# The first expert product of an attention and soft-MoE kernel, moved to a PSUM bank of the output's pool

## The chip, the cores and the metric

The kernel runs on one core of a Trainium2 chip. The metric is the device time of one execution in microseconds (us). The times shown are medians of three runs.

## The reference

The reference is an attention layer whose output goes straight into a soft mixture of experts:

```
# q, k, v: (4, 8, 768, 64); attention in a band of 31 keys, plus 24 block summaries (maximum of k, mean of v)
x = attention(q, k, v)                     # reshaped to (3072, 512)
logits = x @ phi                           # (3072, 32): 8 experts x 4 slots
d = softmax(logits, axis=0); c = softmax(logits, axis=1)
slot_input = d.T @ x                       # (32, 512)
for e in range(8):
    h = maximum(slot_input[4e:4e+4] @ w1[e], 0)    # w1[e]: 512 x 1024
    slot_out[4e:4e+4] = h @ w2[e]                  # w2[e]: 1024 x 512
out = c @ slot_out                         # (3072, 512)
```

All inputs are float32. w1 and w2 are 16 MB each, and the output is 6 MB.

## The kernel before

The program has two parts. The first runs over 24 steps of attention (`for i in range(NSTEP)`); between the steps of attention, pieces of the routing are placed by two tables written out by hand (`PLAN`, and `TAIL` for what follows the last step). Each engine executes its instructions in the order in which the code writes them; the framework adds the waits on semaphores.

In the first part the eight banks of PSUM belong to four pools: `ps_t` (two banks, tag "pt"), `ps_o` (one tile of two banks), `ps_s` (two) and `ps_p` (two). After the last step `att.close()` gives them back. The second part opens two new pools of four banks each, `pf` and then `po`. The banks of `pf` are those of `ps_t` and `ps_o`; the banks of `po` are those of `ps_s` and `ps_p`. The first tile taken from a new pool waits for the instructions that used the old pools whose place it takes.

The end of the first part, in the order of `TAIL`: the last routing sums (`route_d`, accumulated by VectorE into `acc` on line 414); `lanes` (lines 420 to 439), whose last matmul (438) leaves a column in a tile `pp` of `ps_p`; `slots` (441 to 454), which multiplies `acc` into the slot inputs (445), copies them into the stationary operand `W1ST` (449, VectorE) and makes the reciprocal `rz` from the column of line 438 (453, 454); and `row_exp(1)` (457 to 471), which transposes the last two blocks of logits into the tile `o` of `ps_o` (463, TensorE), takes their row maxima (468, VectorE), subtracts them (469, VectorE) and takes the exponent (471, ScalarE).

The second part begins with `row_split` (629 to 638: VectorE and ScalarE make the combine weights `cr`), and beside it the first expert product on TensorE: 32 pieces of w1 of 512 KB each, four matmuls a piece, all accumulated into one tile `hps` (lines 652 to 665). After each piece `load_piece()` issues the DMA of the piece that takes its place, on the queue of SyncE; 43 pieces lie on the chip at that time (`NPRE`), so that pieces 43 to 63 come in while the first 21 are used up. Then follow the maximum with zero (668, 669), transposes of `cr` (`pair_up`, tiles `pc` of `po`) and of the hidden layer (`ph` of `pf`), and a hand-written interleave `ENDING` of the four column blocks of the second product (`stage2`, line 690, tiles `so` and `so2` of `pf`) with the combine (`combine`, line 717, tiles `op` of `po`), whose results VectorE and ScalarE copy to `ot` (726) and SyncE stores (728).

The lines of `slots` and `row_exp` that the prediction speaks of:

```
nc.vector.tensor_copy(out=W1ST..., in_=pi...)                                # 449
nc.vector.tensor_scalar_add(out=rz, in0=ps["z"][:, 0:1], scalar1=EPS)        # 453
nc.vector.reciprocal(out=rz, in_=rz)                                         # 454
nc.tensor.transpose(pv[:, 128 * q : 128 * q + 128], ltq[q0 + q], ident)      # 463
nc.vector.reduce_max(out=cm, in_=lv, axis=AX)                                # 468
nc.vector.tensor_tensor(out=c, in0=lv, in1=cm..., op=ALU.subtract)           # 469
```

Of the kernel before, what the change touches and what calls it, by code (L numbers as in the profile page):

```python
# [9 lines left out]
F32 = mybir.dt.float32  # L10
# [70 lines left out]
def attention_soft_moe(  # L81
# [534 lines left out]
    pf = ctx.enter_context(tc.tile_pool(name="pf", bufs=4, space=PSUM))  # L616
    po = ctx.enter_context(tc.tile_pool(name="po", bufs=4, space=PSUM))
# [11 lines left out]
    def row_split(q0, n):  # L629
        cm = fin.tile([128, 4 * n], F32, name=f"cm{n}", bufs=1)  # L630
        c = lt_all[:, q0 : q0 + n].rearrange("p q (g s) -> p (q g) s", s=NS)
        nc.vector.reduce_sum(out=cm, in_=c, axis=AX)
        nc.vector.tensor_scalar_add(out=cm, in0=cm, scalar1=EPS)
        nc.vector.reciprocal(out=cm, in_=cm)
        nc.vector.tensor_tensor(out=c, in0=c, in1=cm.unsqueeze(2).broadcast_to([128, 4 * n, NS]), op=ALU.mult)
        both = cr[:, 4 * q0 : 4 * q0 + 4 * n]
        nc.scalar.copy(out=both[:, :, 0, :], in_=c)
        nc.vector.tensor_tensor(out=both[:, :, 1, :], in0=c, in1=both[:, :, 0, :].bitcast(F32), op=ALU.subtract)
# [10 lines left out]

    row_split(0, 4)  # L650
    row_split(4, 2)
    hps = pf.tile([128, 512], F32, name="hps", tag="pf")[:, 0:256]
    for k in range(32):
        _, e, c = pieces[k]
        t = wt[k].rearrange("p (j f) -> p j f", j=4)
# [167 lines left out]
```

## Time and profile before

| | |
|---|---|
| median of three runs | 195.24 us (194.88, 195.24, 196.53) |
| the profiled execution: device time | 194.91 us |
| the profiled execution: span of the trace | 193.1 us |
| TensorE busy (matmul) | 169.9 us, 88% of the span |
| VectorE, ScalarE, GpSimd busy | 115.1, 92.1, 78.7 us |
| moved by DMA | 67.64 MB, mean 350 GB/s |

The span runs from the first to the last instruction; the device time holds 1.8 us more. Engines in the profile: PE is TensorE's matmul, PEld its loads of stationary operands, DVE is VectorE, ACT ScalarE, POOL GpSimd, SPq SyncE's queue. "PEclk" is the share of its full clock that TensorE was granted. A row of the timeline has the start, the duration, engine, line, operation, and tiles as output<-inputs; "x8" counts the records that were merged. A float32 matmul leaves two records, so that the 128 matmuls of line 657 are 256 records, eight for each piece of w1. In brackets stands how long the engine was idle before, and what released it; "issue" is idle time in which it waited for nothing that the profile shows.

### The profile page before, as it was taken

The numbers are of one execution on the slowest core, as the hardware profiler recorded it, in microseconds if no ns is written. First come the engines' busy times: TensorE is split into PE (matmuls) and PEld (weight loads), VectorE is DVE, ScalarE is ACT, GpSimd is POOL, SyncE is SP. The second block draws the span as 40 slices with busy tenths as digits, with TensorE's granted clock in tenths as the row PEclk, the third lists the DMA queues.
The fourth block names the chain that finished last, engine by engine and source line by source line (L and its number), as shares of the span: only waits on it lengthen the run. The fifth ranks groups of instructions, "written<-read, shape, count | busy, mean of one in ns | idle before, by whom it ended". The sixth has DMA issues, their size and how long they took to land.

```text
span 193.1 us, 7825 instructions
## 1 busy us (share of the span) xinstructions
PE 169.9 (88%) x3163; PEld 128.7 (67%) x3163; DVE 115.1 (60%) x580; ACT 92.1 (48%) x202; POOL 78.7 (41%) x106
## 2 busy tenths in 40 slices
PE   7779899899799999799989999999879997889950
PEld 5537668677658778578856877876636667768720
DVE  2539959749629958868958867657573020143460
ACT  2036657658464775756686475847220031033440
POOL 2048766856645666576666465860010000000000
PEclk9999999999999999999999999999859999999996
DMA  6999999999998899999899976975959999987696
GB/s 211 351 415 418 416 414 417 419 415 413 404 416 342 277 398 418 410 377 354 247 395 392 392 236 238 311 267 204 333 193 316 417 420 415 416 319 303 259 393 260
DMA packets 19331, 67.64 MB, mean 350 GB/s; under 512 B 2144, under 2 KB 2528, under 8 KB 19296
## 3 DMA queue, kind: packets, MB, share of 16 engines
q1 hardware_dynamic: 19296, 67.15, 90.3%
q8 instruction: 25, 0.41, 0.8%
q14 instruction: 10, 0.08, 0.1%
HBM read 60.85 MB, written 6.29 MB: 348 GB/s over the span
## 4 chain that ended last, share of the span: by engine, by line
PE 60%; DVE 11%; issue 8%; DMA 8%; ACT 5%; POOL 3%; SPq 2%; POOLq 0%; ACTq 0%; DVEq 0%
PE o L309 9%; PE hps L657 8%; PE so L690 8%; DMA v<-vx 8%; PE pt L286 7%; PE s L253 6%; PE pp L208 5%; PE op L717 4%; DVE p L271 3%; DVE kh L184 3%; PE pp L399 2%; PE pp L356 2%; POOL p L275 2%; PE pp L340 2%; PE pp L224 1%
## 5 line engine op out<-in xcount | busy, mean ns | idle before, releaser
L275 POOL TENSOR_TENSOR p<-p,m 128x480 f32<-128x480 f32 x48 | 46.3, 986 | 23.3 <-DVE m L271 22.9
L271 DVE CUSTOM_DVE_ANT_0 p<-s,cs 128x120 f32<-128x120 f32 x192 | 41.0, 278 | 4.9 <-PE s L253 3.5
L280 ACT ACTIVATE p<-p 128x480 f32<-128x480 f32 x48 | 29.0, 608 | 21.8 <-POOL p L275 21.6
L235 POOL COPY v<-vsst 24x520 f32<-24x520 f32 x47 | 29.1, 620 | 20.2 <-issue 17.9
L291 ACT COPY ptr<-pt 120x512 f32<-120x512 f32 x48 | 26.5, 588 | 20.8 <-PE pt L286 20.3
L309 PEld LDWEIGHTS o<-v,ptr 120*64 120x64 f32 x736 | 24.0, 137 | 9.6 <-issue 4.1
L309 PE MATMUL o<-v,ptr 120*64 120x65 f32 x736 | 27.4, 225 | 1.7 <-issue 1.2
L286 PE MATMUL pt<-ident,p 128*120 128x128 f32 x192 | 27.3, 280 | 1.2 <-ACT p L280 1.1
L253 PE MATMUL s<-k,q 64*64 64x120 f32 x768 | 25.9, 269 | 2.1 <-DMA q<-qx 1.2
L253 PEld LDWEIGHTS s<-k,q 64*64 64x64 f32 x768 | 20.3, 133 | 6.1 <-issue 1.7
L286 PEld LDWEIGHTS pt<-ident,p 128*120 128x120 f32 x192 | 20.3, 137 | 6.0 <-ACT p L280 3.3
L184 DVE TENSOR_REDUCE kh<-k 128x30 f32<-128x480 f32 (+1 forms) x32 | 16.1, 545 | 3.4 <-DMA k<-kx 3.4
L657 PE MATMUL hps<-w,W1ST 128*32 128x256 f32 x256 | 15.8, 413 | 1.1 <-DVE lt_all L469 1.1
L329 DVE TENSOR_TENSOR x<-o,z 128x512 f32<-128x512 f32 x23 | 15.9, 691 | 0.8
L271 DVE DVE_READ_ACCUMULATOR2_ANT m<- 128x1 f32 x192 | 15.9, 83 | 0.0
L726 DVE COPY ot<-op 128x512 f32<-128x512 f32 x12 | 7.9, 688 | 11.6 <-PE op L717 11.6
L690 PE MATMUL so<-w,W1ST 128*32 128x128 f32 x256 | 13.4, 275 | 1.0 <-issue 1.0
L657 PEld LDWEIGHTS hps<-w,W1ST 128*32 128x32 f32 x256 | 9.2, 119 | 7.6 <-issue 3.1
L208 PE MATMUL pp<-v,cs 120*32 120x256 f32 x192 | 12.6, 384 | 1.9 <-DMA v<-vx 1.1
L690 PE MATMUL so<-w,W2ST 128*32 128x128 f32 x256 | 13.1, 273 | 0.0
L340 PE MATMUL pp<-ident,x 128*128 128x128 f32 x88 | 12.5, 274 | 0.3 <-ACT xt L346 0.3
L346 ACT COPY xt<-pp 128x512 f32<-128x512 f32 x21 | 12.1, 602 | 0.1
(112 smaller groups left out, 181.2 us busy)
## 6 DMA issues: line engine op xcount, KB each, us to landing
w<-w SPq DMA_DIRECT2D x64, 512.0 KB, 8.9
v<-vx SPq DMA_DIRECT2D x24, 520.0 KB, 7.7
k<-kx SPq DMA_DIRECT2D x16, 472.0 KB, 7.6
q<-qx SPq DMA_DIRECT2D x12, 512.0 KB, 7.0
out<-ot SPq DMA_DIRECT2D x10, 512.0 KB, 3.6
out<-ot SPq DMA_DIRECT2D x4, 256.0 KB, 3.4
cs<-cst SPq DMA_DIRECT2D x1, 288.0 KB, 6.2
self__116<-selx SPq DMA_DIRECT2D x1, 64.0 KB, 5.9
```

The source lines that it names most:

```text
L184: nc.vector.reduce_max(out=kh[:, pr, :, n0 : n0 + m], in_=v[:, :, c0 : c0 + 16 * m].rearrange("p j (m k) -> p j m k", k=16), axis=AX,)
L208: nc.tensor.matmul(pv[32 * g : 32 * g + 32, 0:256], lhsT=cs[0:U, ic : ic + 32], rhs=v[0:U, ab, tt, :, 0:64], start=(tp == 0), stop=(tp == ...
L235: eng.tensor_copy(out=v, in_=src)
L253: nc.tensor.matmul(ps_[i, ab][h : h + 64, u, :], lhsT=qt[i // 2][rows, c : c + 64], rhs=kt[hb, pr][rows, k0 : k0 + U], start=True, stop=Tr ...
L271: nc.vector.tensor_tensor_reduce(out=p[:, n, :], in0=ps_[i, ab][:, 2 * tt + pr, :], in1=maskv[:, mk, :], scale=-0.125, scalar=-NEG, op0=AL ...
L275: nc.gpsimd.tensor_tensor(out=p, in0=p, in1=m.unsqueeze(2).broadcast_to([128, 4, U]), op=ALU.subtract)
L280: nc.scalar.activation(out=p, in_=p, func=AF.Exp, scale=-1.0)
L286: nc.tensor.transpose(pt[:, n, :], p[:, n, :], ident)
L291: nc.scalar.copy(out=ptr, in_=ptr_[i, tt])
L309: nc.tensor.matmul(o[64 * ab : 64 * ab + 64, h, :], lhsT=ptr[:, 2 * pr + ab, 64 * (r ^ ab) : 64 * (r ^ ab) + 64], rhs=v[0:U, ab, tt, h, :] ...
L657: nc.tensor.matmul(hps[32 * j : 32 * j + 32, :], lhsT=W1ST[:, c, 28 * e : 28 * e + 32], rhs=t[:, j, :], start=(k == 0), stop=(k == 31), ti ...
L690: nc.tensor.matmul(so[32 * j : 32 * j + 32, :], lhsT=W2ST[i][:, j, 28 * e : 28 * e + 32], rhs=t[:, i, j, :], start=(e == 0 and i == 0), st ...
```

## The change

The tile `hps`, into which the first expert product accumulates, is taken from the pool `po` (under the tag of the output's tiles) and no longer from `pf`:

```
-    hps = pf.tile([128, 512], F32, name="hps", tag="pf")[:, 0:256]
+    hps = po.tile([128, 512], F32, name="hps", tag="op")[:, 0:256]
```

No instruction is added, removed or moved on any engine. What differs are waits. On TensorE, at the beginning of the first expert product (W1ST is the slot inputs, w_204 the first piece of w1):

```order
 L438 MATMUL pp<-stat,R 128x1 [waits DVE_49,PE_49]
 L463 MATMUL o<-ident,lt_all 128x128 x2
-L657 MATMUL hps<-w_204,W1ST 32x256 [waits DVE_49,PE_49,Pool_49]
+L657 MATMUL hps<-w_204,W1ST 32x256 [waits DVE_49,Pool_49]
 L657 MATMUL hps<-w_204,W1ST 32x256 x3
 L657 MATMUL hps<-w_286,W1ST 32x256 x4
```

The first matmul of the product no longer waits for TensorE's own transposes of line 463 to complete, and its wait for VectorE, which keeps its name, is for another instruction: the count before is reached with line 469, the count now with line 453, three instructions earlier in VectorE's order, which is the same before and after:

```order
540 L414 SCALAR_TENSOR_TENSOR acc<-acc,st,tl 128x256
541 L382 SCALAR_TENSOR_TENSOR stat<-stat,st 128x1
542 L449 COPY W1ST<-tl 128x32x4 [waits DMAHW2_49,DMAHW7_49,PE_49,Pool_49]
543 L453 TENSOR_SCALAR rz<-pp 128x1 [waits PE_49]
544 L454 RECIPROCAL rz<-rz 128x1 [waits DVE_49]
545 L468 TENSOR_REDUCE kh<-o 128x8 [waits PE_49]
546 L469 TENSOR_TENSOR lt_all<-o,kh 128x256 [waits DVE_49]
547 L632 TENSOR_REDUCE cm_2706<-lt_all 128x16 [waits DVE_49]
```

Line 453 is the last reader of a tile of `ps_p`, line 469 the last of a tile of `ps_o`. Later, the tiles of `pf` and `po` fall on other banks by one place in the rotation. On TensorE in the third column block of the combine, this exchanges the waits of two matmuls that follow each other; nothing else differs:

```order
 L717 MATMUL op<-cT,sl 128x512 [waits DVE_49]
 L717 MATMUL op<-cT,sl 128x512
-L717 MATMUL op<-cT,sh 128x512 [waits Activation_49]
-L717 MATMUL op<-cT,sh 128x512 [waits DVE_49]
+L717 MATMUL op<-cT,sh 128x512 [waits DVE_49]
+L717 MATMUL op<-cT,sh 128x512 [waits Activation_49]
 L717 MATMUL op<-cT,sl 128x512 x2
```

## The prediction

> **What bounds the kernel now.** I read the chain that ended last first, then the timeline and the clock around the place of the change, then DMA from there to the end. From the page:
>
> ```profile
> span 193.1 us, 7825 instructions
> PE 60%; DVE 11%; issue 8%; DMA 8%; ACT 5%; POOL 3%; SPq 2%; POOLq 0%; ACTq 0%; DVEq 0%
> ```
>
> TensorE carries the chain. The same chain, cut to the passage into the second part, in order of time (start, duration, what):
>
> ```profile
> 139.36 0.38 PE pp L438 x2
> 139.74 0.54 PE o L463 x2
> 140.28 0.02 issue
> 140.31 0.44 DVE kh L468
> 140.74 0.02 issue
> 140.77 0.44 DVE lt_all L469
> 141.20 0.14 issue
> 141.34 15.82 PE hps L657 x256
> ```
>
> Here the chain leaves TensorE, goes through two VectorE instructions that make softmax weights, and comes back for the expert product. The product reads nothing of what they write. The timeline has the details:
>
> ```profile
> 139.46 0.29 DVE L449 COPY W1ST<-tl 128x128 f32<-128x128 f32 x1 [1.19 <-issue]
> 139.60 0.67 PE L463 MATMUL o<-ident,lt_all 128*128 128x128 f32 x2
> 139.78 0.16 DVE L453 TENSOR_SCALAR rz<-pp 128x1 f32<-128x1 f32 x1
> 140.77 0.42 DVE L469 TENSOR_TENSOR lt_all<-o,kh 128x256 f32<-128x256 f32 x1
> 141.34 1.51 PE L657 MATMUL hps<-w,W1ST 128*32 128x256 f32 x12 [1.07 <-DVE lt_all L469]
> ```
>
> The operand W1ST is ready at 139.46 + 0.29 = 139.75. TensorE ends its transposes at 139.60 + 0.67 = 140.27, stands idle for 1.07 us, and starts when line 469 (done at 141.19) releases it. So this one wait bounds the start.
>
> **What the change takes away.** The product now waits for line 453, done at 139.78 + 0.16 = 139.94. From the end of line 469 to the first matmul it took 141.34 - 141.19 = 0.15; by the same step the release comes at 139.94 + 0.15 = 140.09. TensorE takes its instructions in order, so that the transposes of line 463 are still ahead. Their modelled end is 140.27, but a matmul starts before the end of the one ahead: line 463 began at 139.60, while these rows let line 438 end later.
>
> ```profile
> 139.18 0.57 PE L438 MATMUL pp<-stat,R 128*128 128x1 f32 x2
> ```
>
> It ended at 139.75, 0.15 after its successor's start. With the same overlap the product starts at 140.27 - 0.15 = 140.12; without any, and with the full 0.15 of a release behind the end, at 140.42. I take **140.12**, since the nearest pair of rows shows the overlap: the start moves by 141.34 - 140.12 = **1.22 us** (0.92 to 1.25 by the ends). What is late next is TensorE's own work; line 453 and W1ST are both ahead of it.
>
> **What the gain is worth at the end of the product.** It starts on a slowed clock. Rows of 0.25 us each (stretch, length, PE busy, granted clock, DMA share, GB/s), and the loads of the product:
>
> ```profile
> 138.00:138.25 0.25, 0.25 (x4) 0.91 1.01 410
> ...
> 140.75:141.00 0.25, 0.00 (x0) 0.50 1.06 426
> ...
> 145.00:145.25 0.25, 0.25 (x8) 0.93 0.80 131
> ...
> 189.25:189.50 0.25, 0.00 (x0) 0.81 1.03 426
> ...
> 141.74 0.23 PEld L657 LDWEIGHTS hps<-w,W1ST 128*32 128x32 f32 x4 [0.20 <-issue]
> 142.17 0.22 PEld L657 LDWEIGHTS hps<-w,W1ST 128*32 128x32 f32 x4 [0.20 <-issue]
> ...
> 145.10 11.57 PEld L657 LDWEIGHTS hps<-w,W1ST 128*32 128x32 f32 x216
> ```
>
> The clock drops where a stretch is partly at 1 and partly at 0.5: 0.91 puts the drop 0.205 into its stretch, at 138.205; by the same working the clock comes back at 145.035 and drops again at 189.405. On half clock four records take 142.17 - 141.74 = 0.43, or 0.107 each; on the full one 11.57 / 216 = 0.0536. Before, 141.34 to 145.035 holds 3.70 / 0.107 = 34.5 records, and the other 221.5 take 11.87 us.
>
> So it matters whether the clock's return moves with the start. The three changes lie 6.83 and 44.37 us apart, and 44.37 / 6.83 = 6.50: they fit a beat of 3.41 us, with return and drop on it. If the beat has another phase against the program in every execution, then on the mean over executions the return follows the start of steady work: earlier work finds an earlier beat, and the whole product moves by the full 1.22 us. That is what I take for a median over runs. The times of before fit it: where a beat falls, the slow part is longer by up to 3.41 us, which costs half of that, 1.7 us; the three runs lie 196.53 - 194.88 = 1.65 us apart. The profiled run is at their lower end and had a favourable beat: 145.035 - 3.415 = 141.62, 0.28 us after the product began.
>
> The Trainium skill bears on this: the page "TensorE: Matmul & The Clock Gate", section "What's actually happening", says that the clock is judged over a free-running window of 3413 ns and that one busy window gives the full rate back. The trace agrees with the length (6.83 is twice 3.41). It speaks against counting the whole move in any single run; what it would make of the profiled phase is the first rival.
>
> **From the product to the end.** Everything up to the last matmul follows the product on TensorE. Three things might give the time back. Pieces of w that come too late: SyncE's queue waited for the product itself, so that its DMAs move with it.
>
> ```profile
> SPq L145 <- PE hps L657: 7.3, 9, 4.5
> L145 SPq DMA_DIRECT2D w<-w x29: 327/328/508, 125.9 to 163.4; - x29
> DMA to landing us min/median/max: 3.3/9.0/11.3
> ```
>
> The last piece is issued at 163.4 and lands by 163.4 + 11.3 = 174.7, while the last column block of the second product runs after 177 (row below); the cover is over 2 us, and grows when SyncE issues earlier. The order on SyncE stays, and the outputs queue behind the pieces as now. DMA bandwidth:
>
> ```profile
> 144.00:171.00 27.00, 24.62 (x518) 17.65 (x510) 4.64 (x14) 3.55 (x9) 0.00 (x0) 0.98 1.01 398
> 171.00:177.00 6.00, 6.00 (x144) 4.64 (x142) 2.38 (x6) 2.02 (x5) 0.00 (x0) 1.00 0.77 300
> 177.00:183.00 6.00, 6.00 (x143) 4.64 (x142) 2.49 (x6) 2.05 (x5) 0.00 (x0) 1.00 0.67 268
> 188.00:193.10 5.10, 0.00 (x0) 0.00 (x0) 0.00 (x0) 0.00 (x0) 0.00 (x0) 0.64 0.68 272
> ```
>
> It is full (1.01) while the pieces come, and free for 6 x (0.23 + 0.33) = 3.4 us after them, which is enough for 1.2. The last outputs drain behind the last matmuls, and so move along. Third, TensorE has two stalls whose cause no row names:
>
> ```profile
> 163.73 0.30 PE L690 MATMUL so<-w,W1ST 128*32 128x128 f32 x2 [1.04 <-issue]
> 169.74 0.51 PE L717 MATMUL op<-cT,sl 64*128 64x512 f32 x2 [1.34 <-issue]
> q8 instruction: 1, 0.02, 1.5%
> ```
>
> In the stretch from 160 to 163.8 one packet of the queue for instructions moved (last row). I read both stalls as TensorE waiting for its own code, on DMA that is full of weights. Pieces and product move together, so I leave both at their size; the bounds are that they vanish (a gain of 1.04 + 1.34 = 2.38 more) or that a third one of 1.34 appears; I take nothing, between the two, as the stretch's DMA share is what it was.
>
> The other edits of waits cost nothing: the exchange in the combine stands between two matmuls whose tiles VectorE and ScalarE free in the same pair of copies, and the tiles `ph` and `so` of `pf` come up some 16 us after line 469. VectorE, ScalarE and GpSimd wait for what they waited for before.
>
> **The sum.** Profiled execution: 194.91 - 1.22 = 193.69, with the clock's return moved along. That execution lies 0.33 below the median of 195.24, so for a median I put 195.24 - 1.22 = **194.0 us**.
>
> **The rivals.**
>
> *The clock keeps its beat, and half the gain is lost.* With the return at 145.035 and the start at 140.12, 4.92 / 0.107 = 46.0 records run slowly and the other 210 take 11.26: the end moves from 156.91 to 156.30, a gain of 0.61. Time 194.3 to 194.6 (from the profile and from the median). For it: the beat above. Against: the phase changes, and a median sees many.
>
> *The clock returns a beat earlier.* Before, the beat from 138.2 to 141.62 had an idle stretch of 1.07 us in it and did not bring the clock back. Without that hole TensorE is busy through it. If that is enough, only 1.50 / 0.107 = 14 records are slow, the other 242 take 12.97, and the product ends at 154.59: a gain of 2.32. Time 192.6 to 192.9. Against: line 445's and 438's small matmuls fill half of that beat, and the beat before it, from 134.8, was also busy for two thirds and yet cost the clock.
>
> *The change doesn't do what it says:* the product starts at 141.3 all the same, because a wait that I take for done (W1ST's clearing by GpSimd, the first pieces of w) is not. No row speaks for it. Time 194.9 to 195.2.
>
> *Slower: code comes later.* If the second product reaches its stretches of code earlier than the weights have left DMA, each later stretch adds a stall like the 1.04 and 1.34 above (1.19 in the mean). In the chain, between the two stalls:
>
> ```profile
> 163.73 1.06 PE so L690 x27
> 164.79 0.42 PE so L703 x2
> 165.21 2.76 PE so L690 x96
> 167.97 0.43 PE op L717 x2
> ```
>
> These are 27 + 2 + 96 + 2 = 127 records of matmul; two more such stretches fit into the span before the last matmul, near 175 and 181. Both would cost 2.4, against 1.2 gained: 195.24 + 1.2 = 196.4. It decides where DMA's share at these places is near 1 instead of 0.77 and 0.67. Against: the weights are issued earlier too.
>
> **How the numbers follow.** The forecast 0.45; beat kept 0.22; a beat earlier 0.15; no effect 0.08; code later 0.06; 0.04 for what I don't see. The range reaches from the beat earlier, 192.6, to no effect, 195.3: it leaves out the slower case and the unseen (the stalls gone among it), and allows for where three runs fall on the beat. A change within 1% (1.95 us) can't be told from none here. Faster by more needs 193.29 or less, which is the beat earlier and a little of the forecast's own lower side: 0.18. Slower by over 1% (197.2) needs the code's stalls and a bad beat: 0.03. The rest, 0.79, is within 1%.
>
> **What would show it.** In the profile after, the first matmul of line 657 at 140.1, with no idle time put down to line 469; VectorE's lines 468 and 469 where they were, beside the product; the clock's return somewhere between 141.6 and 147; the product's end near 156 (earlier by what the clock allows); the two stalls still there with 1.0 to 1.4 us; the last copy of line 726 as much earlier as the product's end. I would be wrong if the product began on time and its end did not move, or if the stalls of "issue" grew by as much.

## The result

The changed kernel takes 193.59 us (median of 20 runs, 190.48 to 195.59), the kernel before 195.34 us (20 runs, 192.78 to 197.01): 1.75 us or 0.9% less. The ratio of the two is 0.9865 with a 95% interval of 0.9828 to 0.9901; it is lower than the ratio of the medians (0.9910) because it compares only the executions of each kernel that lie close to its own fastest.

The profiled execution took 192.18 us, 2.73 less than the one before. The chain that ended last, at the same place, in order of time (start, duration, what):

```profile
138.32 0.30 DVE R L434
138.62 0.04 issue
138.67 1.08 PE tl L445 x8
139.75 0.20 PE pp L438 x2
139.94 0.28 PE o L463 x2
140.22 0.12 issue
140.34 14.02 PE hps L657 x256
154.36 1.02 PE pc L645 x8
```

VectorE's lines 468 and 469 are gone from the chain. In the timeline they run beside the product:

```profile
139.81 0.41 PE L463 MATMUL o<-ident,lt_all 128*128 128x128 f32 x2
139.84 0.29 DVE L449 COPY W1ST<-tl 128x128 f32<-128x128 f32 x1 [0.71 <-issue]
140.05 0.15 DVE L453 TENSOR_SCALAR rz<-pp 128x1 f32<-128x1 f32 x1
140.31 5.80 PEld L657 LDWEIGHTS hps<-w,W1ST 128*32 128x32 f32 x112 [0.33 <-issue]
140.75 0.42 DVE L469 TENSOR_TENSOR lt_all<-o,kh 128x256 f32<-128x256 f32 x1
```

Line 453 ends at 140.20, and the first matmul comes 0.14 later, at 140.34, long before line 469 ends at 141.17. Behind the transposes (end 140.22) TensorE now waits 0.12 us; before it waited 1.07. So the wait became 0.95 us shorter.

The larger part of the profile's gain is the clock. The row of the page that gives the granted clock in 40 slices, first of before, then of after:

```profile
PEclk9999999999999999999999999999859999999996
```

```profile
PEclk9999999999999999999999999999999999999995
```

After the change, the 8 and 5 ahead of and in the product are gone: the clock did not drop there at all. Before, it had dropped at 138.2, in work that is the same in both kernels and some 2 us ahead of TensorE's wait, so that this first drop can't be what the change took away. The book of the 2.73 us, from the chains: up to the start of line 434, near the end of the routing, the second execution was 138.32 - 137.45 = 0.87 later; from there to the product it took 140.34 - 138.32 = 2.02 instead of 3.89, which is 1.87 less, 0.95 of it the wait and the rest matmuls ahead of it, at the full clock; the product took 14.02 instead of 15.82, 1.80 less. What follows, up to the last copy, took 0.07 more (last rows of both chains, before and after):

```profile
186.15 0.68 DVE ot L726
```

```profile
183.42 0.68 DVE ot L726
```

In sum, 0.87 - 1.87 - 1.80 + 0.07 = -2.73.

A single profile with such a difference of clock can't say what the change is worth in general; that is what the experiments are for.

### The profile page after: what moved, and what is told of

Same layout as the page of the kernel before. It is cut to its first block, busy times and chain, and to the rows that moved or that the text cites. A ratio compares the mean times of both kernels' runs of the same rounds, so it can differ in the third digit from the quotient of the medians.

```text
span 190.4 us, 7825 instructions
## 1 busy us (share of the span) xinstructions
PE 167.1 (88%) x3163; PEld 128.6 (68%) x3163; DVE 114.9 (60%) x580; ACT 92.1 (48%) x202; POOL 78.8 (41%) x106
## 4 chain that ended last, share of the span: by engine, by line
PE 62%; DVE 12%; DMA 9%; issue 5%; ACT 5%; POOL 2%; SPq 2%; POOLq 0%; ACTq 0%; DVEq 0%
PE o L309 10%; DMA v<-vx 9%; PE so L690 8%; PE s L253 7%; PE hps L657 7%; PE pt L286 7%; PE pp L208 5%; PE op L717 4%; DVE p L271 4%; DVE kh L184 3%; PE pp L399 2%; PE pp L356 2%; PE pp L224 2%; PE pp L340 2%; POOL p L275 2%
## 5 line engine op out<-in xcount | busy, mean ns | idle before, releaser
L657 PE MATMUL hps<-w,W1ST 128*32 128x256 f32 x256 | 14.0, 379 | 0.1
L657 PEld LDWEIGHTS hps<-w,W1ST 128*32 128x32 f32 x256 | 9.9, 110 | 4.0 <-issue 0.3
```

Of the source, the lines that this page charges most:

```text
L657: nc.tensor.matmul(hps[32 * j : 32 * j + 32, :], lhsT=W1ST[:, c, 28 * e : 28 * e + 32], rhs=t[:, j, :], start=(k == 0), stop=(k == 31), ti ...
```

## The experiments

The theory to test: the gain is the wait, released by line 453 (or anything early) and no longer by line 469 ("wait"). Its rival is that the bank itself matters, or the rotation of tiles behind it ("bank"). A second pair asks for the size: whether idle time ahead of the product also costs the clock ("hole", "clock"), or only the start moves ("start alone").

### The wait and the bank, apart

Writing the second half of the row transposes to a tile of `ps_s` turns the two pools' waits round: now `po` has to wait for line 469, and `pf` for no more than the copy of line 449.

```
-        pv = ps["rows"][:, half]
+        pv = ps["rows"][:, 0] if half == 0 else ps_s.tile([128, 512], F32, name="s")
```

With `hps` in `po`, twice:

> hps in a bank of po, but the second half of row_exp's transposes is written to a tile of ps_s, whose place po takes, so that the first expert product waits for line 469 again. Theory 'wait' (the gain is the release by line 453 instead of 469): the product starts about 1.1 us behind the transposes of line 463, with idle time put down to line 469; 195.3 us, as before the change. Theory 'bank' (another bank, or the rotation of the combine's tiles, makes the gain): 193.6 us, as after the change.

> The bank in po with the wait for line 469, again, beside the other two cells. Theory 'wait': clock and time as the kernel before (within 0.5 us of its median). Theory 'bank': as the changed kernel.

Measured: 196.46 us (6 runs; the kernel before 195.69 beside it, 23 runs) and 195.02 us (12 runs; 195.15 before, 35 runs). The bank of the changed kernel brings nothing when the wait is there. TensorE's rows of the second one in the timeline:

```profile
139.97 0.27 PE L463 MATMUL s<-ident,lt_all 128*128 128x128 f32 x1
141.35 0.66 PE L657 MATMUL hps<-w,W1ST 128*32 128x256 f32 x4 [1.10 <-DVE lt_all L469]
```

The idle time put down to line 469 is back, at 1.10 us.

With `hps` in `pf`, as before the change, twice:

> hps in pf as before the change, but the second half of row_exp's transposes is written to a tile of ps_s, so that pf has nothing to wait for behind the copy of line 449. Theory 'wait': the product starts right behind TensorE's transposes of line 463; 193.6 us, as after the change (193.4 to 193.9). Theory 'bank': 195.3 us.

> The bank in pf without the wait for line 469, again, beside the other two cells. Theory 'wait': clock and time as the changed kernel (within 0.5 us of its median). Theory 'bank': as the kernel before.

Measured: 193.22 us (6 runs) and 193.44 us (12 runs; the changed kernel beside it 193.43). The old bank gives the whole gain when the wait is gone. Rows of the second one:

```profile
139.08 0.42 PE L463 MATMUL s<-ident,lt_all 128*128 128x128 f32 x2
139.11 0.29 DVE L449 COPY W1ST<-tl 128x128 f32<-128x128 f32 x1 [0.70 <-issue]
139.46 0.85 PE L657 MATMUL hps<-w,W1ST 128*32 128x256 f32 x12
```

Here the product starts 0.04 us ahead of the transposes' modelled end, right behind them, and 0.06 behind the end of the copy of line 449. All four cells fall as the wait has it, and "bank" is out.

### How large the start alone is

The changed kernel was run once more, beside the others:

> The changed kernel itself, on the chip of the other three. In executions of equal clock it should be 0.9 to 1.1 us faster than before (the start alone); where its median differs by more, the rest is executions that lose the clock for fewer beats. 'Hole': mean clock 0.004 or more above the kernel before, median 1.7 to 2.2 us less. 'Start alone': equal clocks, 1.0 us less.

Measured: 193.43 us (12 runs, mean clock 0.981) against 195.15 (35 runs, 0.977). With each run comes the mean clock that TensorE was granted. A beat of 3.41 us at half clock takes 3.41 x 0.5 / 193 = 0.0088 from that mean, and the runs lie in groups about that far apart, with means of 0.989, 0.981, 0.973 and 0.964. (At the end of every profile, when TensorE has nothing left to do, the clock falls once more; how early moves the mean a little and costs no time.) All runs of the experiments with the wait for line 469 (87 of the kernel before, 18 of `po` with the wait) against all without it (32 of the changed kernel, those of the result among them, and 18 of `pf` without); the clock of the 20 runs of the kernel before in the result is not on record:

| mean granted clock | wait: runs, median us | no wait: runs, median us | difference |
|---|---|---|---|
| 0.984 and over | 10 of 105, 193.18 | 18 of 50, 192.16 | 1.02 |
| 0.977 to 0.983 | 40 of 105, 194.62 | 19 of 50, 193.59 | 1.03 |
| 0.968 to 0.976 | 45 of 105, 195.92 | 10 of 50, 194.91 | 1.01 |
| below 0.967 | 10 of 105, 197.36 | 3 of 50, 196.82 | 0.54 |
| all | 195.33 | 193.51 | 1.82 |

At equal clock the change is worth 1.0 us, in each of the three groups that have runs enough. Within a group and column the runs lie 1.7 to 3.6 us apart, so that an agreement to 0.02 us is in part luck. The other 0.8 us of the median is that executions without the wait lose the clock for fewer beats: 36% of them keep it up to the last matmul against 10%, and 26% are in the two groups of lowest clock against 52%.

The clock also drops in places that the change does not touch. In the profile of this run it stayed up at the product and dropped later (stretches; the granted clock is the third figure from the end):

```profile
168.50:169.00 0.50, 0.50 (x4) 0.39 (x2) 0.50 (x2) 0.50 (x2) 0.00 (x0) 0.78 1.06 434
169.00:172.00 3.00, 3.00 (x52) 2.23 (x50) 0.93 (x3) 0.34 (x1) 0.00 (x0) 0.50 0.74 285
172.00:172.50 0.50, 0.50 (x6) 0.34 (x4) 0.00 (x0) 0.00 (x0) 0.00 (x0) 0.81 1.08 442
```

So the groups of the table mix drops at the product with others.

### Is it the hole that costs the clock?

Matmuls that nothing reads were put into TensorE's idle time. First into four gaps of the routing before the product (`f` is one matmul of 128x256 into a spare bank), in the kernel before and in the changed one:

```
-... R t5 t5 D5 D4 R D5 w w R R D5 L5 S R C1 S C1 C1
+... f R f t5 t5 f f D5 D4 R D5 w w R R D5 L5 f f S R C1 S C1 C1
```

> Before the change, with six matmuls of 128x256 that nothing reads, put into TensorE's idle time between 134 and 138 us. Theory 'clock' (a part of the gain is that TensorE loses its full clock less often or for less time): the clock stays at 1.00 up to the last matmul, about 193.2 us with less scatter, which is the fast group of the changed kernel (192.2) plus one wait of 1.0. Theory 'wait alone': 195.3 us, or some 0.3 more for the added matmuls.

> After the change, with the same six matmuls. Theory 'clock': 192.1 us in nearly all executions, 1.0 to 1.2 less than the kernel before with the same matmuls: that difference is the wait alone. Theory 'wait alone': 193.6 to 193.9 us with the scatter of the changed kernel.

Measured: 196.14 us with the wait and 193.73 us without (12 runs each). Of the runs, 5 of 12 kept the clock with the wait, and 10 of 12 without it. Both are more than without the added work (10 of 105 and 18 of 50), so work in the gaps went with a kept clock, with the hole or without; 5 against 10 of 12 is too few to say what the hole alone does. But the time did not fall, because the added work was not all in idle time. Line 375, which makes the last of the running maxima of the routing, is done when the first added matmul starts. Its row in the changed kernel, and its row and the chain of the same kernel with the added work (the product has line number 666 there):

```profile
135.43 0.16 DVE L375 TENSOR_TENSOR stat<-st,stat 128x1 f32<-128x1 f32 x1
```

```profile
135.04 0.16 DVE L375 TENSOR_TENSOR stat<-st,stat 128x1 f32<-128x1 f32 x1
```

```profile
141.30 14.02 PE hps L666 x256
...
161.94 2.53 PE so L699 x86
164.47 1.39 issue
...
171.77 1.68 issue
```

From line 375 to the product it took 140.34 - 135.43 = 4.91 us without the added work and 141.30 - 135.04 = 6.26 with it: 1.35 us more. The stretch from the product's end to the last copy took another 0.52 us (30.26 against 29.74), with stalls of "issue" of 1.39 and 1.68 instead of 1.09 and 1.34. So the runs that kept the clock have a median of 193.70 with the added work and 192.18 without, and the forecast of 192.1 failed by that. With the wait they have 194.15, against 193.18 without added work; there the stalls were not longer in the profile (1.11 and 1.12), and the forecast of 193.2 failed because the added work took time and 7 of 12 runs lost the clock all the same.

Then into the hole itself, in the kernel before, with two matmuls of 128x512 and with one:

```
+    fb = ps_s.tile([128, 512], F32, name="s")
+    for _ in range(2):                      # one, in the other kernel
+        nc.tensor.matmul(fb, lhsT=ident, rhs=cs[:, 0:512], start=True, stop=True)
     for g in begun.values():
         flush(g)
```

> Before the change (hps in pf, the wait for line 469 kept), with two matmuls of 128x512 that nothing reads, right behind the transposes of line 463, so that TensorE is busy for most of the 1.07 us in which it stood idle. Theory 'hole' (idle time just ahead of the product costs TensorE's clock one more beat of 3.41 us, worth about 1.6 us, on top of the later start): the mean clock rises from 0.974 to about 0.982 as after the change, and the time falls to about 194.3 us (195.7 less 1.4) though the product starts no earlier. Theory 'start alone' (the product takes the clock's return with it): 195.7 us or up to 0.6 more, and the clock as before.

> Before the change with one matmul of 128x512 that nothing reads, behind the transposes of line 463: 0.43 us of TensorE's idle 1.07 us are filled at full clock, 0.86 us at half, so that the product's start never moves. Theory 'hole': fewer executions in the slow groups of the clock than the kernel before in the same runs, and 0.5 to 1 us less time. Theory 'start alone': clock and time as before, within 0.3 us.

Measured: 195.66 us with two (12 runs; 195.21 before, 29 runs) and 195.36 with one (12 runs; 195.15 before). Two matmuls took 1.88 us at full clock, over 0.9 each, where the second expectation counts 0.43. So with two, the work itself kept the product from starting: it began at 142.14, 1.65 behind the end of the transposes.

```profile
140.07 0.42 PE L463 MATMUL o<-ident,lt_all 128*128 128x128 f32 x2
140.32 1.88 PE L610 MATMUL s<-cs,ident 128*128 128x512 f32 x4
142.14 0.64 PE L660 MATMUL hps<-w,W1ST 128*32 128x256 f32 x8
```

One matmul left 0.24 us of idle time and did not move the start:

```profile
139.91 1.02 PE L609 MATMUL s<-cs,ident 128*128 128x512 f32 x2
141.17 0.59 PE L659 MATMUL hps<-w,W1ST 128*32 128x256 f32 x5 [0.24 <-DVE lt_all L469]
```

For "hole": 9 of these 24 runs kept the clock up to the last matmul, against 10 of 105 with the hole empty; and in the profiles, the clock dropped next to the product in all three with the wait and no added work, in none of the three with the wait and added work, and in none of the eight without the wait. Two things qualify this. In two of the first three the clock fell before the hole began (at 138.2, the hole from 140.27; at 140.5, the hole from 141.07), so that the hole can't have caused that drop; what the three share is that the beat with the hole in it was followed by a beat at half clock. And in one of the three with added work, the one with work in the gaps, the hole was still there (1.10 us) and the clock stayed up. The beat with the hole in the kernel before, and in `po` with the wait at its second run (length, PE busy; the granted clock is the third figure from the end):

```profile
138.21:141.62 3.41, 2.34 (x14) 1.89 (x17) 1.91 (x7) 0.31 (x1) 0.28 (x1) 0.50 0.95 359
```

```profile
137.93:141.34 3.41, 1.93 (x18) 1.63 (x15) 2.44 (x10) 0.03 (x1) 0.00 (x0) 1.00 1.01 390
```

TensorE was busy for 2.34 and 1.93 us of these beats (2.35 in the third profile). In the eight profiles without the wait it was busy for about 2.9 us or more of the beat in which the product begins, or that ends where it begins, by beats counted back from the next drop. So the hole may act by what it takes from a beat's work. But busy time in the profile does not decide alone: a beat of 2.47 us (before, from 134.8) and one of 2.67 (`po` with the wait, its first run) ended with a drop, and three of 2.46, 2.46 and 2.53 in other profiles did not.

Against "hole": the medians did not fall, and 5 of the 24 runs are in the group of lowest clock. That an idle hole ahead of the product makes a slow beat there more frequent is likely from these counts; by what rule stays open. That filling it would win time was expected and is not shown.

### The two stalls in the second product

The changed kernel without the loads of pieces 43 to 63; the second product uses the pieces that lie in their places:

```
+        if k >= NPRE:
+            wt[k] = wt[k - NPRE]
+            return
```

> After the change, without the loads of pieces 43 to 63 (the second product uses the pieces that lie in their places). Theory 'code': the two stalls that the profile calls issue (1.09 and 1.34 us) are TensorE waiting for its instructions on DMA that is full of weights; without the loads both go, and the time falls by about 2.4 us to 191.2 us or, with outputs that find DMA free, a little below. Theory 'data': at least the stall in front of line 717, which reads no weights, stays at 1.3 us.

Measured: 190.35 us (4 runs). The chain of the changed kernel in the second product, and the same stretch without the loads:

```profile
156.04 3.85 PE so L690 x133
159.89 1.09 issue
160.99 1.06 PE so L690 x27
162.05 0.42 PE so L703 x2
162.47 2.76 PE so L690 x96
165.23 0.43 PE op L717 x2
165.66 1.34 issue
167.00 0.98 PE op L717 x6
```

```profile
157.00 4.52 PE so L693 x160
161.51 0.42 PE so L706 x2
161.93 2.76 PE so L693 x96
164.69 1.12 PE op L720 x8
```

Both stalls are gone, the one ahead of the combine included, which reads no piece of w. "Data" can't explain that one. The stretch from 156.04 to 167.98 is 3.13 us longer than the same work without the loads (157.00 to 165.81); the stalls are 2.43 of it, and the matmuls around them the rest.

The other profiles show what the stalls belong to. Counting TensorE's matmul records along the chain from the first of line 657, the two stalls come after these counts (some records can be missing from a trace):

| | records added ahead of the product | first stall after | second stall after |
|---|---|---|---|
| nine profiles without added matmuls | 0 | 403 | 529 to 531 |
| one matmul in the hole | 2 | 400 | 528 |
| two matmuls in the hole | 4 | 398 | 526 |
| six in the gaps, with and without the wait | 12 | 518 | 646 |

With 12 records added, one stall comes 12 records earlier than the second one did, the other 128 records behind it, in the middle of other blocks of matmuls; the one due near 391 is missing. So the stalls follow the count of TensorE's instructions, in steps of about 128 matmul records with as many loads, and not what a matmul reads. Together with the run without loads, that speaks for TensorE waiting for its code on full DMA; the wait itself is in no row.

### Transposes moved into a gap

The transposes of line 463 were moved ahead of line 445, where TensorE waits for line 434; first in the changed kernel, then with `hps` in `pf` and the rows in `ps_s`:

```
-... w w R R D5 L5 S R C1 S C1 C1
+... w w R C1 R D5 L5 S R S C1 C1
```

> After the change, with the two transposes of line 463 moved ahead of the matmuls of line 445, into TensorE's idle time there (0.4 us), and lines 468 and 469 behind line 454. Theory 'hole': no later start of the product (W1ST and line 453 end when they did) and a little less idle time, so 0.9 or more of the executions in the two faster groups of the clock: 193.0 to 193.4 us. Theory 'start alone': 193.6 us, since the start is held by lines 449 and 453 and does not move.

> hps in pf, the second half of row_exp's transposes in a tile of ps_s and moved ahead of line 445: the product waits for line 449 alone. Theory 'wait': 193.2 us, as with the transposes where they were, since line 449's copy is then what the start waits for (about 0.5 us behind line 445's end in either order); 'start alone' with the transposes' 0.3 us taken out of TensorE's way: 192.9 us.

Measured: 192.44 us (12 runs) and 191.98 us (12 runs), against 195.21 before beside them (29 runs): both lie below every time that was forecast. The first keeps the start of the changed kernel (1.67 us from line 445 to the product, in both), and at the kept clock it takes as long (192.00 against 192.18); its median is 1.2 us lower than 193.59 because 7 of its 12 runs kept the clock and none is in the two groups of lowest clock. That is the direction of "hole", but 7 of 12 against 11 of 32 is too few to tell. The chain of the second:

```profile
138.10 0.34 PE tl L445 x2
138.44 0.13 DVE stat L382
138.57 0.71 issue
139.27 0.30 DVE W1ST L449
139.57 0.04 issue
139.62 14.02 PE hps L657 x256
```

From line 445 to the product it takes 1.52 us, in the changed kernel 140.34 - 138.67 = 1.67: the start is 0.15 earlier, and is now held by line 449, the copy that the product really needs. At the full clock (9 of 12 runs, median 191.75) it is 0.4 us ahead of the changed kernel (192.18, 11 of 32 runs). Against the kernel before its ratio is 0.9903 (0.9859 to 0.9946), and it is the fastest version of this study that loads all the weights, by its median; the changed kernel was not run beside it, so that how far it is ahead of that is not shown.

## Why the prediction was right, and where it was off

The forecast was 194.0 us, the range 192.6 to 195.3, and a change within 1%; 193.59 us and -0.9% came out.

**The wait.** Right in kind: the product was held by line 469 and nothing else, and the early release gives the gain whichever bank it is in. The step "the start moves by 1.22" was too large: 0.95 by the wait in the profile, 1.0 us at equal clock. What failed is "what is late next is TensorE's own work; line 453 and W1ST are both ahead of it". I had that from a profile in which the transposes ran at half clock, and let the product start 0.15 ahead of their end. At full clock they end sooner (0.41 us instead of 0.67 from start to end), and line 453 is late next: the product starts with its release, 0.12 behind the transposes' end, and in `pf` without that wait 0.04 ahead of it, where it follows W1ST.

**The clock.** The step "the clock's return moves along with the start", by which the clock adds nothing, failed: the executions without the wait lose it for fewer beats, worth about 0.8 us of the median. The rival "the clock returns a beat earlier", at 0.15, had the right direction, and its reading that a beat with the hole in it is followed by a slow one fits all three profiles with the wait and no added work; it gave 192.6 to 192.9 for a case that is only part of the runs. "The beat kept, and half the gain lost" is not seen: at equal clock the gain is 1.0, not 0.61. In sum the gain was put at 1.22 instead of 1.75; the median of before came out 0.1 higher than the one I started from, so that 194.0 is 0.4 too high. That it came so near is in part luck: a start put 0.2 too large made up for some of the clock's 0.8 that was left out.

**From the product to the end.** Right: from the product's end to the last copy the profiles took 29.67 and 29.74 us, and the two stalls stayed at 1.09 and 1.34 (1.04 and 1.34 before). The slower rival, a third stall of code, did not come; the reading behind it is supported by the run without loads and by the stalls' fixed count of instructions, though no row shows the wait for code itself.

**What decides the scatter.** The prediction gave the spread of 1.65 us in the three runs of before to the beat's phase alone. The Trainium skill ("TensorE: Matmul & The Clock Gate", section "What's actually happening") gives the window by which the clock is judged as 3413 ns; the groups of the mean clock, about 0.008 apart where such a window takes 0.0088, are near it. But the drops are not all in one place: in single profiles the clock dropped for one beat near 50 us, for one or two next to the product, and for one near 169 us. What brings it down at the first and the last of these was not tried.

## What to carry to other kernels

When pools are closed and opened in the middle of a kernel, the first tile of a new pool inherits the last readers of the place it takes; look in the chain for an engine that is released by an instruction whose result it never reads, and give the first tile of the next stage the place that comes free first. Moving the late reader's tile does as well as moving the waiting one. Where the clock of TensorE scatters, compare runs at equal clock: here that gave 1.0 us in three groups, while medians of few runs mixed it with the clock.

## What was not expected of the hardware

Idle time of about 1.1 us ahead of a long product went with one or two beats of 3.41 us at half clock next to it in all three profiles that had it without added work, and work that filled most of it went with none in two; over all runs 10% kept the clock with the wait and 36% without. TensorE's two stalls of 1.1 and 1.3 us with no releaser vanished when DMA had no weights to load, and when 12 matmul records were added ahead of them, they came at other matmuls, after 518 and 646 records of the product and what follows instead of 403 and 530. Their length varies without such work too: the second took 1.12 to 1.63 us in nine profiles without added matmuls, and 1.12 to 1.87 in four with them.
